# Dealing out VectorE work and moving loads and evictions in an FNet + GEGLU kernel on one core

## The chip, the cores and the metric

One core of one Trainium2 chip runs the kernel. The time is device microseconds for one execution. The profile is of another single execution on the same kind of core, and its times are microseconds from the start of its span. TensorE multiplies matrices; VectorE and ScalarE are the two engines that read its results out of PSUM; GpSimd does elementwise work on SBUF alone; SyncE and GpSimd also issue the transfers. Each engine works through its own instructions in order and waits for the others by semaphores.

## What is computed

`x` has 2048 rows (S) of 448 numbers (D). After a layer norm, `xn` goes two ways, and the two results are multiplied and added to `x`:

```python
xn = _layernorm(x)
a = einsum("bsd,ed->bse", xn, dft_hid_re)          # DFT along D, real part
b = einsum("bsd,ed->bse", xn, dft_hid_im)          # and imaginary part
s = einsum("ts,bse->bte", dft_seq_re, a) - einsum("ts,bse->bte", dft_seq_im, b)
g = silu((gelu(xn @ w_gate) * (xn @ w_up)) @ w_down)     # F = 1792
return x + s * g
```

## The kernel before

All is float32, but each operand is split for TensorE into a high part (rounded to the matmul's type) and a low part (the rest), so that a product takes two or three matmuls. `split` (L141) is that step: ScalarE copies the high part, VectorE subtracts it from the source. Several products are done as seven block products instead of eight, so that sums and differences of blocks have to be made first, of `x`, of weights and of DFT matrices.

The order is written out by hand (`tc.manual_schedule()`, L510): the order of the lines is the order on each engine. The stages:

1. **Start and first group of F, to 80 us.** `x` comes in four chunks c = 0..3 of 512 rows. For each, `stats` (L149) makes mean and variance on VectorE and ends with four tiny steps (`newton`, L164 to L170) on which `norm` waits; `turn_mm` (L184) transposes the normalized rows on TensorE, and `turn_split` (L196) brings them back as high part, low part (VectorE, L202) and a full copy `xf` (ScalarE, L201). With the first two blocks of F plain products are made: `gateup` (L388), `act`, and `down` (L423), whose results leave PSUM through ScalarE (L416, `po_out`) in two PSUM banks. `between` is a list of steps put between the four parts of a `down`.
2. **Combinations.** `combine(p, s)` (L207) makes from the `xf` blocks of a pair p of chunks (c = 2p and 2p+1) the four differences that the seven-product form needs: one memset and four subtractions of 128x512 per call, in place, each waiting for the one before. `t_places` and `v_places` (L221, L234) split them into tiles `t_lo` and `t_v`. For pair 0 both calls stand after the first `gateup` with all of c = 2 (L719), for pair 1 in the first unit of the next stage (L789).
3. **Twelve more blocks of F, 80 to 415 us.** `strassen` (L441) is one unit: a block of F with a pair of chunks, seven products into four PSUM banks `x1`..`x4`, with VectorE and ScalarE steps in between, and with lists of other steps (`preps`, and `dn` for pieces of the `down` of earlier units) at four places. `sums_s` (L291) makes the ten sums of a block's weights on GpSimd; its input comes by `load_s`, and `prep_s` splits the result. The first such weight block is loaded at L616, ahead of most of the start. `spill` and `fetch` write half of the transposed chunks 1 and 3 to DRAM, because `t_places` writes over them, and bring them back later. The summed results of the F blocks are kept in DRAM (`gs`), added there by transfers that GpSimd issues (L421).
4. **DFT along D, 415 to 492 us.** For each block k of 128 rows, in the order 0..13, 15, 14, `hid_mm` (L904) makes 22 matmuls into two PSUM banks. Eight banks are in turn, so that TensorE can be four blocks ahead. `hid_sums` (L928) evicts the two banks on ScalarE (L933, L934) into one of two buffers (`f_at`, L896: `a_t` for even k, `a_r[0]` for odd) and makes four sums on VectorE (L939 to L942); `hid_split` (L946) splits 128x1568 from there into the block's place `AT[k]` (ScalarE L951, VectorE L954). It is put off by one block (`behind`) up to k = 10 and done at once after that. Blocks 10 and 15 (`KP`) are only split (`hid_plain`, L919). In the same stage the four chunks of `gs` are fetched through the two halves of `a_st`, put through silu on ScalarE and stored back (L1038 to L1045): fetch of one chunk, in the next block its silu, its store, and the fetch of another. The first DFT matrices for the next stage are loaded by `load_c` (L982), summed by `sum_c` (VectorE, L1000 and L1001) and split by `prep_c` (L1005); the buffers of units 1 and 2 are the two halves of `a_r[0]`.
5. **DFT along S and output, 492 us to the end.** 112 units of 14 matmuls (`seven`, L1087) and 16 plain ones. Unit 0 begins when `hid_mm(14)` is through and uses the eight banks in the order in which `hid_mm` gave them back.

SyncE issues most loads in order, so a load whose buffer isn't free holds up those behind it.

Of the kernel before, what the change touches and what calls it, by code (L numbers as in the profile page):

```python
# [13 lines left out]
P = 128  # L14
S = 2048
D = 448
# [29 lines left out]
def fnet_geglu(ctx: ExitStack, tc: tile.TileContext, x, ca, ct, cp, et, wgu, wd, out):  # L46
# [66 lines left out]
    t_hl, t_lo, vt = [None, None], [], [None, None]  # L113
# [93 lines left out]
    def combine(p, s):  # L207


        (b11, b21), (b12, b22) = [  # L210
            [xfk(c, 2 * s + k) for k in range(2)] for c in (2 * p, 2 * p + 1)
        ]
        if s == 1:
            nc.gpsimd.memset(b22[64:], 0.0)
        nc.vector.tensor_sub(b11, b12, b11)
        nc.vector.tensor_sub(b12, b22, b12)
        nc.vector.tensor_sub(b22, b22, b11)
        n = 64 if s else P
        nc.vector.tensor_sub(b21[:n], b21[:n], b22[:n])

    def t_places(p):  # L221
# [4 lines left out]
        t_hl[p] = [list(zip(h, l)), None]  # L226
# [283 lines left out]
    with tc.manual_schedule():  # L510
# [105 lines left out]
        s_raw = load_s(GROUPS[1][0], 1)  # L616
# [33 lines left out]
        between = [lambda k=k: turn_split(*turn_mm(2, k)) for k in (1, 2, 3)]  # L650
        turn = between[0]
        between[0] = lambda: (turn(), l0())
# [15 lines left out]
        xp = [dram.tile([P, 2, 1024], F32, name=f"xp{p}") for p in range(2)]  # L668

        def x_half(p):  # L670
            return a_x[2 * p + 1].rearrange("p (a d) -> p a d", a=2)[:, :, :1024].bitcast(F32)

        def spill(p):
            nc.sync.dma_start(xp[p], x_half(p))

        def fetch(p):
            nc.sync.dma_start(x_half(p), xp[p])

# [3 lines left out]
        for c in (2, 3):  # L682
            if c == 2:
                draw = load_d(GROUPS[1], a_st[:, 2304:])
                spill(0)
# [3 lines left out]
            if c == 2:  # L689
# [3 lines left out]
                    lambda: (l0(), norm(3), turn(0)),  # L693
                    lambda: turn(1),
                    lambda: turn(2),
                ]
                between1 = [lambda: turn(3)]
                sums_s(s_raw, nc.gpsimd)
            else:
# [7 lines left out]
                v_split = v_places(0)  # L707
                between1 = [lambda: v_split(1), lambda: v_split(2)]
# [7 lines left out]
            if c == 2:  # L716
                h1()
                l1()
                combine(0, 0)  # L719
                combine(0, 1)  # L720
# [54 lines left out]
        for gi in range(1, len(GROUPS)):  # L775
# [7 lines left out]
            for bi, (i, p) in enumerate(zip((0, 1, 1, 0), sides)):  # L783
                preps = [[], [], [], []]
                if gi == 1 and bi == 0:
                    preps[0].append(lambda: (v_split(0), v_split(3)))
                if gi == 1 and bi < 2:
                    if bi == 0:
                        preps[1].append(lambda: combine(1, 0))  # L789
                        preps[3].append(lambda: combine(1, 1))  # L790
                    else:
                        tsp, vsp = t_places(1), v_places(1)
                        for n in range(4):
                            preps[n].append(lambda n=n: (tsp(n), vsp(n)))
# [14 lines left out]
                elif bi == 1:  # L809
                    if nxt:  # L810
# [4 lines left out]
                        else:  # L815
                            wdn, steps = prep_d(grp, draw)
                            for f in steps:
                                preps[0].append(f)
# [44 lines left out]
        def place(tag, n):  # L863
# [14 lines left out]
            7: lambda: a_x[0],  # L878
# [3 lines left out]
            12: lambda: a_x[1],  # L882
            13: lambda: place("st", 8 * D),
# [12 lines left out]
        def f_at(k):  # L896
            return (a_t if k % 2 == 0 else a_r[0])[:, : 8 * HD]
# [76 lines left out]
        def slot_at(m):  # L974
            return (
                lambda: (a_d[0][1], rest(a_x[0])),
# [41 lines left out]
        for k in [*range(14), 15, 14]:  # L1018
# [4 lines left out]
            if k == 14:  # L1023
                break
            if k in KP:
                hid_plain(k, ps, [rest(v) for v in ((vt[0], t_lo[0]), a_x[1:3])[k > 10]])
# [4 lines left out]
            if k not in KP:  # L1031
                behind.append(lambda k=k: hid_split(k)())
                if k > 10:
# [4 lines left out]
            for n, c in enumerate((2, 3, 0, 1)):  # L1038
                at = (3, 4, 6, 7)[n]
                if k == at:  # L1040
                    g_in[c] = stage(c)
                    nc.sync.dma_start(g_in[c], gv[:, 4 * c : 4 * c + 4])
                if k == at + 1:
                    nc.scalar.activation(g_in[c], g_in[c], AF.Silu)
                    nc.sync.dma_start(gv[:, 4 * c : 4 * c + 4], g_in[c])  # L1045
            if k == 8:
# [5 lines left out]
            if k == 13:  # L1052
                load_c(1)
                load_c(2)
                sum_c(3)
# [230 lines left out]
```

## Time and profile before

| | us |
|---|---|
| median of 3 runs (lowest, highest) | 803.74 (801.69, 804.31) |
| the profiled execution, whole | 805.21 |
| its span in the profile | 803.5 |
| TensorE matmuls busy | 773.8 |
| VectorE busy | 548.2 |
| ScalarE busy | 363.8 |
| GpSimd busy, DMA issues included | 175.7 |

TensorE has work nearly all the time, so what counts is where it is idle, and where its granted clock is below full: after some of the idle stretches it is 0.5 for a few microseconds. The transfers move 170 MB at 212 GB/s in the mean. A row of the timeline gives start, duration, engine, line, operation and tiles, and in brackets how long the engine had been idle and what ended that. Engine names in the rows: PE is TensorE, DVE VectorE, ACT ScalarE, POOL GpSimd, SP SyncE.

### The profile page before, as it was taken

The page shows a single profiled execution, that of the slowest core. Times are in us where ns is not written, and L with a number is a line of the kernel's source. Part 1 is how long each engine was busy: PE and PEld are TensorE (multiplying, and loading weights), DVE is VectorE, ACT ScalarE, POOL GpSimd, SP SyncE. Part 2 cuts the span into 40 slices and gives each one's busy share as a digit, 9 for nine tenths or more (in the row PEclk, how much of TensorE's full clock was granted, in tenths as well). Part 3 has the DMA queues.
Part 4 walks back from the last instruction along what each step waited for, and adds up shares of the span by engine and source line. Part 5 has one row for each costly group of instructions (what it writes and reads, how often), then busy time and mean ns, then how long its engine had stood idle before and what let it go on. Part 6 is the DMA issues. An engine that isn't in the chain of part 4 may idle for free. (4 is left out here: it accounts for less than half of the span.)

```text
span 803.5 us, 11376 instructions
## 1 busy us (share of the span) xinstructions
PE 773.8 (96%) x4044; PEld 692.5 (86%) x4044; DVE 548.2 (68%) x945; ACT 363.8 (45%) x538; POOL 175.7 (22%) x300
## 2 busy tenths in 40 slices
PE   9898899999999999999999996899999999999997
PEld 7787788888888888888889995799999999888996
DVE  7877778555565556455544546779787796969687
ACT  3684355344434444343444654444343444344341
POOL 2103006240321512401011000213232322213130
PEclk9999999999999999999999998799999999999999
DMA  8042445995878968865989860777796969596884
GB/s 307 12 161 112 163 136 151 269 203 119 235 142 219 276 115 230 172 138 110 300 173 262 340 258 17 230 271 235 270 309 209 343 196 360 177 314 210 292 246 187
DMA packets 61370, 170.05 MB, mean 212 GB/s; under 512 B 7424, under 2 KB 40064, under 8 KB 60416
## 3 DMA queue, kind: packets, MB, share of 16 engines
q1 hardware_dynamic: 47440, 108.17, 38.4%
q0 software_dynamic: 13728, 61.02, 33.1%
q8 instruction: 32, 0.52, 0.3%
q14 instruction: 26, 0.21, 0.1%
q10 hardware_dynamic: 144, 0.11, 0.0%
HBM read 127.21 MB, written 70.91 MB: 247 GB/s over the span
## 5 line engine op out<-in xcount | busy, mean ns | idle before, releaser
L432 PE MATMUL x<-xt,w 128*128 128x512 f32 x480 | 150.0, 393 | 3.0 <-DVE tmp L493 2.6
L432 PEld LDWEIGHTS x<-xt,w 128*128 128x128 f32 x480 | 90.5, 189 | 20.0 <-DVE tmp L493 3.0
L416 ACT ACTIVATE po_out<-po 128x448 f32<-128x448 f32 x112 | 60.1, 537 | 83.2 <-PE po L409 79.2
L409 PE MATMUL po<-wd0h,hs 128*128 128x448 f32 x256 | 82.7, 370 | 2.3 <-ACT po_out L416 2.3
L421 POOL DMA_DIRECT2D gs<-po_out x24 | 21.4, 890 | 218.8 <-ACT po_out L416 213.8
L915 PE MATMUL ab<-e,xt 128*128 128x448 f32 x288 | 68.8, 365 | 0.0
L409 PE MATMUL po<-wd,hs 128*128 128x448 f32 x288 | 66.0, 365 | 0.0
L432 PE MATMUL x<-t_v,w 128*128 128x512 f32 x216 | 61.1, 391 | 0.0
L409 PEld LDWEIGHTS po<-wd,hs 128*128 128x128 f32 x288 | 54.1, 188 | 6.6
L915 PEld LDWEIGHTS ab<-e,xt 128*128 128x128 f32 x288 | 54.1, 188 | 4.3
L409 PEld LDWEIGHTS po<-wd0h,hs 128*128 128x128 f32 x256 | 48.7, 190 | 7.7 <-ACT po_out L416 2.7
L1093 PE MATMUL p<-t_v,wd0l 128*128 128x448 f32 x112 | 39.3, 393 | 13.6 <-DVE xt L143 5.8
L994 POOL DMA_DIRECT2D raw<-sums x45 | 24.8, 551 | 110.3 <-DVE raw_d L1000 38.5
L432 PEld LDWEIGHTS x<-t_v,w 128*128 128x128 f32 x216 | 40.5, 188 | 8.8 <-DVE t_v L143 0.2
L409 PE MATMUL po<-wd0l,hs 128*128 128x448 f32 x128 | 47.4, 370 | 0.0
L142 ACT ACTIVATE e<-raw 128x896 fp32r<-128x896 f32 (+1 forms) x30 | 27.6, 921 | 36.9 <-DVE raw L1001 29.4
L487 ACT ACTIVATE hs<-tmp 128x512 fp32r<-128x512 f32 x24 | 15.2, 634 | 56.9 <-DVE tmp L485 56.9
L1093 PE MATMUL p<-w,e 128*128 128x448 f32 x112 | 38.6, 390 | 0.9 <-DMA w<-td 0.8
L432 PE MATMUL x<-t_lo,w 128*128 128x512 f32 x96 | 37.4, 389 | 0.0
L1093 PEld LDWEIGHTS p<-t_v,wd0l 128*128 128x128 f32 x112 | 21.4, 191 | 18.2 <-DVE xt L143 6.3
L1093 PE MATMUL p<-xt,e 128*128 128x448 f32 x112 | 36.1, 374 | 0.0
L994 POOL DMA_DIRECT2D tmp<-sums x39 | 21.4, 550 | 63.7 <-DVE xt L143 28.7
(298 smaller groups left out, 2007.1 us busy)
## 6 DMA issues: line engine op xcount, KB each, us to landing
gs<-po_out POOLq DMA_DIRECT2D x24, 896.0 KB, 8.5
sums<-ca SPq DMA_DIRECT2D x16, 896.0 KB, 10.7
sums<-ca POOLq DMA_DIRECT2D x16, 896.0 KB, 14.6
t_v<-td SPq DMA_DIRECT2D x24, 448.0 KB, 5.6
w<-td SPq DMA_DIRECT2D x24, 448.0 KB, 7.4
raw<-ct SPq DMA_DIRECT2D x45, 192.0 KB, 4.7
raw<-wgu SPq DMA_DIRECT2D x12, 640.0 KB, 4.2
tmp<-ct SPq DMA_DIRECT2D x39, 192.0 KB, 4.9
```

The source lines that it names most:

```text
L142: nc.scalar.activation(h, src, AF.Copy)
L409: nc.tensor.matmul(po[:, :D], hs[:, a, kk * P : (kk + 1) * P], wdn[b][:, i], start=n == 0, stop=n == 5,)
L416: nc.scalar.activation(out_[0][:, kk], po[:, :D], AF.Copy)
L421: nc.gpsimd.dma_start(gv[:, 4 * c : 4 * c + 4], out_[0], accum_op=ALU.add)
L432: nc.tensor.matmul(ps, a[i], b[j], start=first and n == 0, stop=n == 2, skip_group_check=True)
L487: nc.scalar.activation(hs[:, 0], g1, AF.Copy)
L915: nc.tensor.matmul(p[:, :D], a, b, start=n == 0, stop=n == len(mm) - 1)
L994: nc.gpsimd.dma_start(v[:, 4 * P : 6 * P], sums[j][:, KS.index(k)])
L1093: nc.tensor.matmul(ps[q][:, :D], h, v, start=u % UN == 0, stop=False, skip_group_check=True)
```

## The change

Three parts, in one diff.

- **Combinations.** `combine` now takes an engine and returns four steps. Pair 0 stays on VectorE, but its eight steps are taken one by one (`comb.pop(0)()`), after each of the turns of chunk 2 (k = 1, 2, 3) and chunk 3, the last one after `l1`. Pair 1 goes to GpSimd as a whole, at the head of the first unit, the s = 1 half first. The splits that follow are dealt out anew: those of pair 0 all before the first unit, those of pair 1 one at a time over the first two units and the head of the third.
- **Weight sums later.** `load_s` of the first summed weight block and its `sums_s` on GpSimd move from the start to behind `spill(0)`, just before the first `down`; `spill(0)` itself moves there from the third chunk.
- **End of the DFT-along-D stage.** The four chunks of `gs` get a place each (two in `a_st`, two in `g_in` over the tile of `x` chunk 0) and are fetched at k = 3, 4, 4, 5, with the silu three blocks later (6, 7, 7, 8). `load_c(0)` moves from k = 8 to k = 3. Block 13 uses buffer `a_t` instead of `a_r[0]`, block 11 is split one block later, blocks 12 and 13 change places in the tiles, and the loads of units 1 and 2 move from k = 13 to k = 12, with `sum_c(1)` ahead of block 15's split.

```diff
-    def combine(p, s):
+    def combine(p, s, eng):
...
+        def first_():
+            if s == 1:
+                nc.gpsimd.memset(b22[64:], 0.0)
+            eng.tensor_sub(b11, b12, b11)
+
+        return [
+            first_,
+            lambda: eng.tensor_sub(b12, b22, b12),
+            lambda: eng.tensor_sub(b22, b22, b11),
+            lambda: eng.tensor_sub(b21[:n], b21[:n], b22[:n]),
+        ]
...
         d_low()
-        s_raw = load_s(GROUPS[1][0], 1)
         load_x(3, 0, 4)
...
+        spill(0)
+        s_raw = load_s(GROUPS[1][0], 1)
+        sums_s(s_raw, nc.gpsimd)
+        comb = combine(0, 0, nc.vector) + combine(0, 1, nc.vector)
+
+        def turn2(k):
+            turn_split(*turn_mm(2, k))
+            if k == 1:
+                l0()
+            comb.pop(0)()
...
-                    lambda: (l0(), norm(3), turn(0)),
-                    lambda: turn(1),
-                    lambda: turn(2),
+                    lambda: (l0(), norm(3), turn(0), comb.pop(0)()),
+                    lambda: (turn(1), comb.pop(0)()),
+                    lambda: (turn(2), comb.pop(0)()),
                 ]
-                between1 = [lambda: turn(3)]
-                sums_s(s_raw, nc.gpsimd)
+                between1 = [lambda: (turn(3), comb.pop(0)())]
...
-                v_split = v_places(0)
-                between1 = [lambda: v_split(1), lambda: v_split(2)]
+                between1 = [lambda: v_split(0), lambda: v_split(3)]
...
-                combine(0, 0)
-                combine(0, 1)
+                comb.pop(0)()
+                v_split = v_places(0)
+                v_split(1)
+                v_split(2)
...
                 if gi == 1 and bi == 0:
-                    preps[0].append(lambda: (v_split(0), v_split(3)))
-                if gi == 1 and bi < 2:
-                    if bi == 0:
-                        preps[1].append(lambda: combine(1, 0))
-                        preps[3].append(lambda: combine(1, 1))
-                    else:
-                        tsp, vsp = t_places(1), v_places(1)
-                        for n in range(4):
-                            preps[n].append(lambda n=n: (tsp(n), vsp(n)))
+                    for f in combine(1, 1, nc.gpsimd) + combine(1, 0, nc.gpsimd):
+                        f()
+                    tsp, vsp = t_places(1), v_places(1)
+                    preps[0].append(lambda: vsp(3))
+                    preps[3].append(lambda: (vsp(1), tsp(1)))
+                if gi == 1 and bi == 1:
+                    for n, f, k in ((0, tsp, 2), (1, vsp, 2), (2, tsp, 0), (3, vsp, 0)):
+                        preps[n].append(lambda f=f, k=k: f(k))
+                if gi == 1 and bi == 2:
+                    tsp(3)
...
-            return (a_t if k % 2 == 0 else a_r[0])[:, : 8 * HD]
+            return (a_t if k % 2 == 0 or k > 12 else a_r[0])[:, : 8 * HD]
...
+            if k == 13:
+                behind.pop(0)()
+            if k == 15:
+                sum_c(1)
...
                 behind.append(lambda k=k: hid_split(k)())
-                if k > 10:
+                if k == 13:
                     behind.pop()()
...
-            for n, c in enumerate((2, 3, 0, 1)):
-                at = (3, 4, 6, 7)[n]
+            if k == 4:
+                x0 = sb.tile([P, 4096], F32, name="g_in", tag="x0")
+            for c, at, v in ((2, 3, (a_st, 0)), (3, 4, None), (0, 4, None), (1, 5, (a_st, 1))):
                 if k == at:
-                    g_in[c] = stage(c)
+                    v, i = v or (x0, int(c == 0))
+                    g_in[c] = part(v, 4 * D * i, 4, D)
                     nc.sync.dma_start(g_in[c], gv[:, 4 * c : 4 * c + 4])
-                if k == at + 1:
+                if k == at + 3:
                     nc.scalar.activation(g_in[c], g_in[c], AF.Silu)
                     nc.sync.dma_start(gv[:, 4 * c : 4 * c + 4], g_in[c])
-            if k == 8:
+            if k == 3:
                 raw_d0 = sb.tile([P, 2 * D], F32, name="raw_d0", tag="d0h")
                 load_c(0)
...
-            if k == 13:
+            if k == 12:
                 load_c(1)
                 load_c(2)
+            if k == 13:
                 sum_c(3)
...
-        sum_c(1)
         prep_c(1)
```

The first place is VectorE from the last turn of chunk 3 on; `xf_72` holds the blocks of pair 0, and the row with `gu_3_1` is the multiplication that the first `gateup` of chunk 3 waits for. Before:

```order
L202 TENSOR_TENSOR xt_69<-pt_3_661,xt_69 128x2x2x128
L383 TENSOR_TENSOR tmp<-tmp,gu_2_1_649 128x512
L385 TENSOR_TENSOR hs_79<-tmp,hs_79 128x512
L215 TENSOR_TENSOR xf_72<-xf_72 128x512
L216 TENSOR_TENSOR xf_72<-xf_72 128x512
L217 TENSOR_TENSOR xf_72<-xf_72 128x512
L219 TENSOR_TENSOR xf_72<-xf_72 128x512
L215 TENSOR_TENSOR xf_72<-xf_72 128x512
L216 TENSOR_TENSOR xf_72<-xf_72 128x512
L217 TENSOR_TENSOR xf_72<-xf_72 128x512
L219 TENSOR_TENSOR xf_72<-xf_72 64x512
L383 TENSOR_TENSOR tmp<-tmp,gu_3_1_696 128x512
```

The same place on VectorE now:

```order
L202 TENSOR_TENSOR xt_69<-pt_3_668,xt_69 128x2x2x128
L223 TENSOR_TENSOR xf_72<-xf_72 128x512
L389 TENSOR_TENSOR tmp<-tmp,gu_2_1_656 128x512
L391 TENSOR_TENSOR hs_79<-tmp,hs_79 128x512
L224 TENSOR_TENSOR xf_72<-xf_72 64x512
L143 TENSOR_TENSOR t_v_694<-xf_72,t_v_694 128x512 x2
L389 TENSOR_TENSOR tmp<-tmp,gu_3_1_701 128x512
```

Six of the eight combinations of pair 0 have gone to earlier places, and two splits stand ahead of the multiplication that stood behind it.

The second place is GpSimd behind the first weight sums, where `raw_74`, `xf_83` and `po_out` hold the blocks of pair 1 and `raw_75` the second weight block; now:

```order
L217 MEMSET xf_72 64x512
L217 MEMSET po_out 64x512
L218 TENSOR_TENSOR xf_83<-raw_74,xf_83 128x512
L222 TENSOR_TENSOR raw_74<-po_out,raw_74 128x512
L223 TENSOR_TENSOR po_out<-po_out,xf_83 128x512
L224 TENSOR_TENSOR xf_83<-xf_83,po_out 64x512
L218 TENSOR_TENSOR xf_83<-raw_74,xf_83 128x512
L222 TENSOR_TENSOR raw_74<-raw_74 128x512
L223 TENSOR_TENSOR raw_74<-raw_74,xf_83 128x512
L224 TENSOR_TENSOR xf_83<-xf_83,raw_74 128x512
L303 TENSOR_TENSOR raw_75<-raw_75 128x128
```

Before, the row of the weight sums followed the first memset directly; now eight subtractions stand ahead of it.

The third place is ScalarE at the end of the DFT-along-D stage, from block 11 to unit 1 (`raw_74` and `tmp` are the two buffers, `e_3015<-raw_74` is the split of unit 1's matrices). Before:

```order
L933 ACTIVATE raw_74<-ab_0_3654 128x2x224
L934 ACTIVATE raw_74<-ab_1_3666 128x2x224
L951 ACTIVATE xt_68<-raw_74 128x7x224
L933 ACTIVATE tmp<-ab_0_3686 128x2x224
L934 ACTIVATE tmp<-ab_1_3698 128x2x224
L951 ACTIVATE xt_67<-tmp 128x7x224
L933 ACTIVATE raw_74<-ab_0_3718 128x2x224
L934 ACTIVATE raw_74<-ab_1_3730 128x2x224
L951 ACTIVATE ts_st<-raw_74 128x7x224
L142 ACTIVATE xt_67<-ab_0_3757 128x448
L922 ACTIVATE xt_68<-ab_1_3769 128x448
L142 ACTIVATE e_3015<-raw_74 128x896
```

The same place on ScalarE now:

```order
L946 ACTIVATE raw_74<-ab_0_3655 128x2x224
L947 ACTIVATE raw_74<-ab_1_3667 128x2x224
L946 ACTIVATE tmp<-ab_0_3685 128x2x224
L947 ACTIVATE tmp<-ab_1_3697 128x2x224
L964 ACTIVATE xt_68<-raw_74 128x7x224
L964 ACTIVATE ts_st<-tmp 128x7x224
L946 ACTIVATE tmp<-ab_0_3721 128x2x224
L947 ACTIVATE tmp<-ab_1_3733 128x2x224
L964 ACTIVATE ts_x_3754<-tmp 128x7x224
L142 ACTIVATE ts_x_3754<-ab_0_3759 128x448
L935 ACTIVATE xt_68<-ab_1_3771 128x448
L142 ACTIVATE e_3015<-raw_74 128x896
```

Block 12 is evicted ahead of block 11's split, block 13 goes through `tmp` behind block 12, and so `raw_74` is given up for the loads of units 1 and 2 with block 11's split instead of block 13's.

42 lines of the change are left out of this document (16 added, 26 removed).

## The prediction

> **What bounds the kernel now.** I read the page first, then who TensorE waited for, then the stretches around those waits. The page's busy line and the waits of TensorE:
>
> ```profile
> PE 773.8 (96%) x4044; PEld 692.5 (86%) x4044; DVE 548.2 (68%) x945; ACT 363.8 (45%) x538; POOL 175.7 (22%) x300
> ...
> PE p L1093 <- DVE xt L143: 5.8, 1, 5.8
> PE p L1093 <- ACT tmp L933: 3.0, 1, 3.0
> PE pt L187 <- issue: 2.7, 1, 2.7
> PE x L432 <- DVE tmp L493: 2.6, 1, 2.6
> ...
> PE po L409 <- ACT po_out L416: 2.3, 1, 2.3
> PE p L1093 <- ACT raw L933: 2.1, 1, 2.1
> ```
>
> TensorE is the bound: 803.5 less 773.8 leaves some 30 us idle, and these six single waits are 18.5 of them. A wait can cost more than itself, since matmuls behind it can run at a lower clock. The stretches (duration, then busy us of PE, PEld, DVE, ACT, POOL, then PEclk):
>
> ```profile
> 20.70:23.60 2.90, 0.18 (x2) 0.10 (x2) 2.86 (x3) 0.72 (x1) 2.74 (x7) 1.00 0.05 14
> 23.60:28.70 5.10, 5.09 (x30) 4.88 (x31) 3.95 (x7) 2.90 (x5) 0.14 (x1) 0.67 0.00 0
> 67.70:75.10 7.40, 5.06 (x25) 4.36 (x24) 6.01 (x9) 3.48 (x7) 5.99 (x9) 1.00 0.00 0
> 94.30:98.40 4.10, 1.54 (x8) 0.96 (x6) 3.81 (x6) 0.08 (x1) 0.00 (x0) 1.00 0.30 124
> 98.40:104.00 5.60, 5.54 (x17) 4.33 (x17) 4.79 (x7) 5.36 (x11) 0.00 (x0) 0.70 0.02 4
> 414.00:492.30 78.30, 78.30 (x388) 72.58 (x387) 38.95 (x63) 41.30 (x51) 6.50 (x10) 1.00 0.79 244
> 492.30:516.60 24.30, 13.31 (x58) 11.37 (x58) 16.22 (x31) 11.10 (x14) 4.92 (x9) 0.65 0.36 110
> 516.60:572.00 55.40, 55.40 (x349) 52.74 (x348) 45.47 (x86) 24.32 (x27) 13.87 (x24) 1.00 0.85 287
> ```
>
> There are four holes: at 21, 72, 96 and 492 us. The one at 492, where the DFT along S begins, is by far the largest. At 55.40 / 349 = 0.159 us a matmul, its 58 matmuls need 9.2 us, and they took 24.3: 15.1 us lost, 11.0 of it idle and the rest at PEclk 0.5 to 0.65.
>
> **Part 1: the end of the DFT along D (gain 14.5).** TensorE itself never waits in 414 to 492; it runs ahead through eight banks while ScalarE falls behind. What holds ScalarE, and what that leads to at the end:
>
> ```profile
> ACT po_out L1044 <- DMA po_out<-gs: 12.9, 3, 6.5
> ...
> 477.49 0.53 ACT L933 ACTIVATE raw<-ab 128x448 f32<-128x448 f32 x1
> ...
> 485.86 0.53 ACT L933 ACTIVATE raw<-ab 128x448 f32<-128x448 f32 x1
> ...
> 488.50 1.52 ACT L951 ACTIVATE xt<-raw 128x1568 fp32r<-128x1568 f32 x1 [1.69 <-DVE raw L942]
> 489.93 0.52 ACT L933 ACTIVATE tmp<-ab 128x448 f32<-128x448 f32 x1
> ...
> 494.68 0.53 ACT L933 ACTIVATE raw<-ab 128x448 f32<-128x448 f32 x1
> ...
> 499.43 0.53 ACT L142 ACTIVATE xt<-ab 128x448 fp32r<-128x448 f32 x1
> ...
> 505.54 0.95 ACT L142 ACTIVATE e<-raw 128x896 fp32r<-128x896 f32 x1 [5.16 <-DVE raw L1001]
> 506.40 0.53 ACT L933 ACTIVATE tmp<-ab 128x448 f32<-128x448 f32 x1
> ...
> 465.57 0.77 PE L915 MATMUL ab<-e,xt 128*128 128x448 f32 x3
> ...
> 499.55 1.79 DVE L954 TENSOR_TENSOR ts_st<-raw,ts_st 128x1568 fp32r<-128x1568 f32 x1 [1.62 <-ACT ts_st L951]
> ```
>
> The silus wait 12.9 us for their fetches, each of which stands behind the store of the chunk before. Block 9, which TensorE finished at 465.57 (block 10 begins there), is evicted at 477.49: 11.9 us late. In the tail blocks 11, 12, 13 and 15 follow 4.1 to 4.8 us apart, no faster than TensorE makes them (78.30 / 388 = 0.202 us a matmul, 4.4 for the 22 of a block), so nothing is caught up. Then unit 1's matrices can only be loaded when block 13's split has left `raw` (499.55 + 1.79 = 501.3), their split stands until 505.54, and block 14's eviction is queued behind it, at 506.40. Unit 0 needs those banks.
>
> After the change the four fetches go out together. The one into slot 0 of `a_st` waits for the last accumulation, issued at 431.0, and the others stand behind it on SyncE, with `load_c(0)`:
>
> ```profile
> L421 POOL DMA_DIRECT2D gs<-po_out x24: 859/878/1041, 131.2 to 431.0; - x24
> ...
> DMA to landing us min/median/max: 7.1/8.5/15.4
> ```
>
> That landing is at 438 to 446. Four chunks of 0.92 MB at the 244 GB/s of this stage take 15 us, at full engines less: they are there by 453 to 461, and the silus stand behind the evictions of blocks 6, 7, 7 and 8 (455 to 465). So little of the 12.9 is left. ScalarE then loses only the table load and the second silu of block 7, some 2.8 us, and regains a part at block 10: I take 2 us late at block 9 instead of 11.9. From there by durations: block 11 evicted at 476.7, block 12 at 479.7 (TensorE makes it by 478.9), VectorE's lows of 11 and 12 at 482.9 and 484.7, loads of units 1 and 2 out at 483 instead of 501.4, block 13 through `tmp` by 490.3, block 15's lows by 492.5, unit 1's split at 492.5 to 494.6, block 14's eviction at 493.4 to 494.3. TensorE starts unit 0 at 492.3, needs block 15's banks at 493.6 and block 14's at 494.2, and unit 1 at 494.5: about 0.5 us is left of the 15.1. Units 4 and 5 load at 492.4, as soon as `e1` is free, and have the 56 x 0.159 = 8.9 us of units 0 to 3 for it. Gain 14.5, at worst 7 if fetches or the loads of units 1 and 2 come late. The new places and the exchange of blocks 12 and 13 change no duration.
>
> **Part 2: weight sums later (gain 3.4).** The tiny steps ahead of chunk 1's norm, and the same step where GpSimd is idle:
>
> ```profile
> 20.62 2.02 DVE L170 SCALAR_TENSOR_TENSOR sd<-sd 128x4 f32<-128x4 f32 x1
> ...
> 38.08 0.17 DVE L170 SCALAR_TENSOR_TENSOR sd<-sd 128x4 f32<-128x4 f32 x1
> ```
>
> L170 took 2.02 instead of 0.17 us while GpSimd ran the sums (2.74 busy in 20.70:23.60), on the path to the transposes. With the sums gone the hole shrinks by 1.85, and by 0.25 of its neighbours, to 0.6, and the clock of 0.67 over the next 5.1 us (1.7 us) should stay up. The sum is 3.8; I take 3.4, as the splits of chunk 1 come close to TensorE then. The sums now run behind `spill(0)`, by my estimate from about 36 on, beside work on VectorE that has some slack; what they cost there is in part 3.
>
> **Part 3: the combinations, hole at 72 (loss 1.0) and hole at 96 (gain 4.2).** At 72 `po` waits for ScalarE, which waits for a VectorE multiplication (L383) behind the eight combinations. VectorE from the first combination on, with two later rows of it; the one GpSimd subtraction of this size class; the stretch to which six combinations go; and ScalarE around the split of the second weight sums:
>
> ```profile
> 64.93 0.68 DVE L215 TENSOR_TENSOR xf<-xf 128x512 f32<-128x512 f32 x1
> ...
> 67.99 0.95 DVE L215 TENSOR_TENSOR xf<-xf 128x512 f32<-128x512 f32 x1
> ...
> 71.47 0.67 DVE L383 TENSOR_TENSOR tmp<-tmp,gu 128x512 f32<-128x512 f32 x1
> ...
> 97.62 0.67 DVE L493 TENSOR_TENSOR tmp<-tmp,x 128x512 f32<-128x512 f32 x1
> ...
> 128.03 2.26 DVE L503 TENSOR_TENSOR hs<-tmp,hs 128x512 fp32r<-128x512 f32 x1
> ...
> 72.17 0.63 ACT L384 ACTIVATE hs<-tmp 128x512 fp32r<-128x512 f32 x1 [2.56 <-DVE tmp L383]
> ...
> 8.49 1.85 POOL L279 TENSOR_TENSOR w<-raw,w 128x768 fp32r<-128x768 f32 x1 [7.17 <-DVE w L276]
> ...
> 40.00:62.70 22.70, 22.70 (x120) 19.54 (x119) 17.35 (x36) 19.68 (x39) 0.00 (x0) 1.00 0.41 148
> ...
> 83.78 0.94 ACT L315 ACTIVATE w<-raw 128x896 fp32r<-128x896 f32 x1
> 87.13 0.55 ACT L416 ACTIVATE po_out<-po 128x448 f32<-128x448 f32 x1 [2.40 <-issue]
> ```
>
> Eight took 71.47 - 64.93 = 6.5, 0.82 each; six go (-4.9), two splits come (+1.3). But the six now stand in 40 to 62.7, where VectorE has 22.70 - 17.35 = 5.4 us of idle for their 4.1, not always at the right place: its lows of chunks 2 and 3 slip by 0.5 to 2, which TensorE feels as some 1.4, and the multiplication gains less. From 62 GpSimd runs pair 1: 8 instructions of 128x512, by L279 at 1.85 x 512/768 = 1.24 us each, 10 us, longer with contention. Beside 128x128 sums a VectorE subtraction takes 0.95 instead of 0.68 in one place and 2.26 in another (L503), so a price from 0.3 to 1.6 each. About five stand ahead of the multiplication; I take 0.5 each, near the dense case, where VectorE always had the next one ready, as here. The wait at 72 stays at about 2.0 of 2.3; less 1.3 for the slips: -1.0, from +2 to -6.
>
> By the Trainium skill's page SBUF — State Buffer, section Who interferes with whom, a VectorE instruction with two SBUF inputs and a GpSimd instruction that reads SBUF shut each other out for a whole instruction. L503 agrees with it, the 0.95 at 67.99 less so; by that rule the five would wait up to 1.24 each and this part would be near its lower end.
>
> At 96 the hole waits for L493 at 97.62. VectorE has ten instructions fewer ahead of it in the first unit (eight combinations, two splits) and three splits more: 7 x 0.68 = 4.8 us earlier, against a hole of 2.6. Contention eats at most part of it, as GpSimd should be through by then. So the 2.6 go, and with them 0.30 of the 5.6 us behind at PEclk 0.70, 1.7: 4.2 us. The second weight sums now end on GpSimd at 82 to 86 by these prices; ScalarE's split of them (83.78) has 2.40 us of idle behind it. The later `tsp(3)` delays one load of `wd` by about 1 us, which may cost 0.3.
>
> The clock terms in parts 2 and 3 are 3.4 together. The Trainium skill's page TensorE: Matmul & The Clock Gate, section What's actually happening, gives an idle window of some 3.4 us before the clock halves; holes of 2.7 and 2.6 us did it here, so the rows decide. By that rule alone these terms could fail and the result would be about 786.
>
> **Sum.** 14.5 + 3.4 - 1.0 + 4.2 - 0.3 = 20.8 us. The profiled execution (805.21, span 803.5) would come to 784.4; it lay 1.5 above the median of 803.74, which gives 783.0.
>
> **Rivals.**
> - *GpSimd blocks VectorE in 62 to 86.* For it: L170 and L503. Against it: the dense case. Each blocked instruction pays 1.3 or more, the hole at 72 grows to 6 or 7 us with its clock loss, and 6 us of the gain go: 789. Chance 0.17.
> - *The end of the DFT along D stays bound.* If four fetches at once beside the `td` stores land after 465, or VectorE's chain through blocks 11 to 15 is longer than drawn, half of part 1 goes: 790. For it: a DMA share of 0.79 there, over 1.0 in single slices. Chance 0.14.
> - *Slower than before.* The same lock, but on all of the some 16 VectorE instructions with two SBUF inputs in 62 to 90, each at the 1.6 of L503, all on the path: 25 us against 20.8, so 808. It decides from 1.3 each with none hidden; VectorE has several microseconds of idle there. Chance 0.03.
> - *The hole at 72 closes as well* and the slips are hidden: 779. Chance 0.06.
> - *No change worth measuring*: TensorE could be held by something else at 492, such as the first loads. Nothing shows that. Chance 0.03.
>
> **Numbers.** The forecast has 0.57. The range goes from 777 (part 3 at +2, no remainder in parts 1 and 2) to 792 (either of the first two rivals and a bit more). 0.3% is 2.4 us, about what a measurement of this kernel can tell from no change. Faster 0.94, same 0.03, slower 0.03.
>
> **What would show it.** Right: no idle of ScalarE at the silus, PEclk at full from 485 to 520 and under 2 us idle there; L170 ahead of chunk 1 at 0.17; no hole in the first unit. Wrong: ScalarE still over 6 us behind at block 9, or a wait of TensorE over 4 us in 60 to 90 behind VectorE subtractions that take over 1.5 us.

## The result and the profile after

The kernel after takes 783.58 us (median of 4 runs, 782.86 to 784.53) against 802.72 (800.11 to 804.31): the ratio is 0.9765, with a 95% interval of 0.9734 to 0.9797. Its profiled execution took 782.91, with a span of 781.1. That is 22.4 us less span than in the profile before. The medians lie only 19.1 apart, since the profiled execution before was 2.5 above its median and the one after 0.7 below; by the ratio it is 18.9.

The busy line of the page after, and the largest waits of TensorE:

```profile
PE 766.0 (98%) x4044; PEld 686.4 (88%) x4044; DVE 545.3 (70%) x937; ACT 363.8 (47%) x538; POOL 189.1 (24%) x308
```

```profile
PE p L1112 <- DVE cc L1209: 3.6, 4, 1.0
PE po L415 <- ACT po_out L422: 3.1, 1, 3.1
...
PE pt L187 <- issue: 0.4, 1, 0.4
```

Of the six single waits before, five are gone or down to 0.4. The one for `po_out` at 72 us has grown, from 2.3 to 3.1. The stretches that answer to those of before (duration, then busy us of PE, PEld, DVE, ACT, POOL, then PEclk):

```profile
23.60:28.70 5.10, 4.98 (x38) 4.50 (x37) 3.84 (x7) 3.92 (x8) 0.00 (x0) 1.00 0.00 2
...
72.20:76.00 3.80, 3.80 (x18) 3.25 (x19) 3.80 (x5) 3.45 (x7) 3.80 (x6) 1.00 0.26 109
...
485.60:494.60 9.00, 9.00 (x57) 8.31 (x57) 6.49 (x13) 5.31 (x8) 3.09 (x6) 1.00 0.60 182
```

The start of the last stage has no idle at all now (9.00 of 9.00, clock 1.00), and the clock behind the first transposes of chunk 1 is full. Where the 22.4 came from is seen by setting the start of each TensorE instruction against that of the same instruction before (the order is the same). This lead, with the times of before, is 3.4 us at instruction 133 (27.55), 2.4 ahead of the hole at 72 and 1.7 at its end, 6.3 behind the hole at 96, 6.8 at 131, 21.9 at 511 and 22.4 at the end.

ScalarE at the silus and at the end of the DFT along D:

```profile
452.62 3.29 ACT L1063 ACTIVATE g_in<-g_in 128x1792 f32<-128x1792 f32 x2
...
458.05 1.71 ACT L1063 ACTIVATE po_out<-po_out 128x1792 f32<-128x1792 f32 x1
460.10 0.55 ACT L946 ACTIVATE raw<-ab 128x448 f32<-128x448 f32 x1 [0.33 <-DVE xt L967]
...
485.43 0.95 ACT L142 ACTIVATE e<-raw 128x896 fp32r<-128x896 f32 x1 [3.01 <-PE ab L928]
486.29 0.53 ACT L946 ACTIVATE tmp<-ab 128x448 f32<-128x448 f32 x1
```

No silu waits for its fetch. Block 9, finished by TensorE at 458.7, is evicted at 460.10, 1.4 us late. Before, 11.9. At 485.43 ScalarE waits for TensorE, whose matmuls of block 14 read `e` until then: ScalarE is no longer the one that is late.

Around the hole at 72, VectorE and GpSimd:

```profile
60.51 1.18 DVE L223 TENSOR_TENSOR xf<-xf 128x512 f32<-128x512 f32 x1
...
62.99 1.77 DVE L391 TENSOR_TENSOR hs<-tmp,hs 128x512 fp32r<-128x512 f32 x1 [0.70 <-ACT hs L390]
64.69 1.78 DVE L224 TENSOR_TENSOR xf<-xf 64x512 f32<-64x512 f32 x1
66.40 3.46 DVE L143 TENSOR_TENSOR t_v<-xf,t_v 128x512 fp32r<-128x512 f32 x2
69.79 0.67 DVE L389 TENSOR_TENSOR tmp<-tmp,gu 128x512 f32<-128x512 f32 x1
```

```profile
61.23 1.62 POOL L222 TENSOR_TENSOR raw<-po_out,raw 128x512 f32<-128x512 f32 x1
64.30 1.62 POOL L224 TENSOR_TENSOR xf<-xf,po_out 64x512 f32<-64x512 f32 x1
```

Four VectorE instructions with two SBUF inputs take 1.77 us instead of 0.69 beside GpSimd's. The multiplication at 69.79, which reads one input from PSUM, takes its usual 0.67.

### The profile page after: what moved, and what is told of

It reads as the page before. It is cut to its first block, busy times and chain, and to the rows that moved or that the text cites. A ratio compares the mean times of both kernels' runs of the same rounds, so it can differ in the third digit from the quotient of the medians.

```text
span 781.1 us, 11376 instructions
## 1 busy us (share of the span) xinstructions
PE 766.0 (98%) x4044; PEld 686.4 (88%) x4044; DVE 545.3 (70%) x937; ACT 363.8 (47%) x538; POOL 189.1 (24%) x308
## 4 chain that ended last, share of the span: by engine, by line
PE 69%; DVE 15%; DMA 10%; issue 3%; ACT 1%; SPq 0%; DVEq 0%; ACTq 0%
PE x L438 23%; PE po L415 16%; PE ab L928 9%; PE p L1112 8%; PE x L445 4%; PE p L1115 4%; DVE xt L143 4%; DVE e L143 3%; DMA w<-td 3%; PE gu L361 3%; DMA raw<-ct 2%; DMA tmp<-ct 2%; DMA raw<-wgu 1%; DMA raw_d<-ct 1%; DVE cc L1150 1%
## 5 line engine op out<-in xcount | busy, mean ns | idle before, releaser
L1112 PE MATMUL p<-t_v,wd0l 128*128 128x448 f32 x112 | 37.5, 380 | 3.6 <-DVE cc L1209 3.6
L1112 PE MATMUL p<-w,e 128*128 128x448 f32 x112 | 36.6, 375 | 0.1
L323 DVE TENSOR_TENSOR w<-raw,w 128x512 fp32r<-128x512 f32 (+1 forms) x24 | 21.3, 889 | 19.9 <-ACT w L321 19.9
L143 DVE TENSOR_TENSOR e<-raw,e 128x896 fp32r<-128x896 f32 (+1 forms) x30 | 31.4, 1047 | 4.3 <-ACT e L142 4.0
## 6 DMA issues: line engine op xcount, KB each, us to landing
sums<-ca POOLq DMA_DIRECT2D x16, 896.0 KB, 14.5
```

What stands on the lines that cost most here:

```text
L143: nc.vector.tensor_sub(l, src, h)
L1112: nc.tensor.matmul(ps[q][:, :D], h, v, start=u % UN == 0, stop=False, skip_group_check=True)
```

## The experiments

The theory after the result: three parts that add up, and a hole at 72 that is left because GpSimd holds up VectorE there (the lock: while GpSimd is in an instruction that reads SBUF, one of VectorE's with two SBUF inputs has to stand, and the other way round). All kernels in one table; the ratio is to the kernel before on the same chip, with its 95% interval.

| run | what | median us | ratio |
|---|---|---|---|
| e1_dend | before + end of DFT along D | 791.20 | 0.9847 (0.9819 to 0.9875) |
| e2_sums | before + weight sums later | 799.87 | 0.9950 (0.9928 to 0.9973) |
| e3_comb | before + combinations | 800.24 | 0.9961 (0.9943 to 0.9980) |
| e6_fetch | after, old order at the end of D | 787.41 | 0.9793 (0.9764 to 0.9823) |
| e7_tail | after, old fetches | 792.29 | 0.9859 (0.9834 to 0.9884) |
| e4_dve | after, pair 1 on VectorE | 783.26 | 0.9761 (0.9741 to 0.9782) |
| e5_sumsfirst | after, second weight sums first | 779.65 | 0.9722 (0.9699 to 0.9744) |
| e8_halves | after, GpSimd in halves | 779.03 | 0.9705 (0.9678 to 0.9731) |
| e5_again | e5_sumsfirst again | 781.76 | 0.9717 (0.9693 to 0.9741) |
| after_again | after again | 783.88 | 0.9765 (0.9739 to 0.9790) |
| e9_chain | after, halves in a chain | 782.11 | 0.9760 (0.9735 to 0.9785) |
| e10_both | sums first, halves in a chain | 779.53 | 0.9719 (0.9699 to 0.9740) |

### Each part alone

**e1_dend**: only the hunks of the diff from `AT` on.

> The kernel before with the part on the end of the DFT along D alone. Theory (three parts that add up: 15.1 us here, 3.4 for the weight sums, some 2.7 net for the combinations): 15.1 us faster than before, and the holes at 21, 72 and 96 us as they were. Rival (the parts need each other, as part 1 gets its slack from an earlier start): under 12 or over 18 us.

TensorE's waits, and the stretch from where the last stage begins:

```profile
PE x L432 <- DVE tmp L493: 2.5, 1, 2.5
PE po L409 <- ACT po_out L416: 2.4, 1, 2.4
PE pt L187 <- issue: 2.2, 1, 2.2
```

```profile
492.00:516.60 24.60, 24.60 (x157) 23.20 (x156) 21.55 (x41) 14.39 (x17) 6.45 (x12) 1.00 0.81 269
```

The first three holes stand as they did, and the fourth is shut without any lead from the earlier stages: 157 matmuls where 58 ran in a stretch of about that length before. Against the trace of before the lead is 0.35 ahead of the hole, 15.1 at 511 and 15.5 just behind it. The ratio gives 12.3 (10.0 to 14.5): of the difference, 2.0 is that the profiled execution before lay above the median of 803.21 of its 23 runs in this comparison, and 1.4 is given back in the last stage. That the parts need each other is not borne out by the trace; the interval of the time alone would reach below the rival's 12.

**e2_sums**: `load_s`, `sums_s` and `spill(0)` moved as in the diff, the rest as before.

> The kernel before with the weight sums and the spill later, and nothing else. Theory: 3.4 us faster, L170 ahead of chunk 1 at 0.17 us, the TensorE clock in 23 to 28 us at full; with the sums now beside VectorE in 36 to 60 us nothing shows on TensorE there. Rival (the sums only move their contention to the later stretch): L170 at 0.17, but 1 us or more is lost again before 72 us, and the gain is under 2.4 us.

The last tiny step ahead of chunk 1's norm on VectorE, and the stretch from the transposes on:

```profile
20.11 0.17 DVE L170 SCALAR_TENSOR_TENSOR sd<-sd 128x4 f32<-128x4 f32 x1
```

```profile
21.00:26.10 5.10, 4.98 (x39) 4.51 (x40) 3.81 (x7) 3.40 (x7) 0.00 (x0) 1.00 0.00 2
```

L170 is back at 0.17 and the clock at 1.00. The lead is 3.8 at the instruction that stood at 27.55 before, 3.6 at 41 and 3.4 from 60 to 97, with the sums running at 35.5 to 40.4: at most 0.3 was given back there. By the ratio 4.0 us (2.2 to 5.8). One thing more stands in this trace: behind the hole at 96 (2.54 here) the clock stayed full, and then TensorE waited 1.69 for VectorE's L471, at 100.67. The lead is 3.4 on both sides of it, so what the halved clock cost there before was lost to VectorE here: in the first unit VectorE sets the pace.

**e3_comb**: only the combinations and splits, with the steps of `prep_d` one place later (an edit of the whole change that the diff above leaves out).

> The kernel before with the combinations and splits dealt out anew and pair 1 on GpSimd; the weight sums and the end of the DFT along D as before. Theory: 2.7 us faster (4.5 from the hole at 96, 1.8 lost before it), the wait at 72 us about 3.1 with VectorE's instructions of 128x512 at 1.77 us there. Rival (the loss before 72 comes from the weight sums that now run beside VectorE, not from the combinations): 4 us or more faster and a wait at 72 of 2.3 or less.

The wait of TensorE at 72:

```profile
PE po L415 <- ACT po_out L422: 3.1, 1, 3.1
```

3.1 us faster (1.6 to 4.6) by the ratio, with the wait at 72 at 3.1 and none in the first unit. So the growth of that hole belongs to the combinations, not to the weight sums beside VectorE. The three gains, 12.3 + 4.0 + 3.1 = 19.4, add up to the 18.9 of the whole change, well within their intervals.

### The end of the DFT along D: fetches or order

**e6_fetch** keeps the four places, the early `load_c(0)` and the new tiles of the blocks, and takes back the rest of that part:

```diff
-            return (a_t if k % 2 == 0 or k > 12 else a_r[0])[:, : 8 * HD]
+            return (a_t if k % 2 == 0 else a_r[0])[:, : 8 * HD]
...
-            if k == 13:
-                behind.pop(0)()
-            if k == 15:
-                sum_c(1)
...
-                if k == 13:
+                if k > 10:
                     behind.pop()()
...
-            if k == 12:
+            if k == 13:
                 load_c(1)
                 load_c(2)
...
         load_c(5)
+        sum_c(1)
         prep_c(1)
```

> The kernel after, but of its edits to the DFT along D only the fetch into four places is kept: block 13 in the second buffer, blocks 11 and 12 split at once, the loads of units 1 and 2 and the sum for unit 1 where they were before. Theory (being on time on ScalarE carries part 1, and the order at the end is a finish): 2 to 4 us slower than the kernel after, so 15.5 to 17.5 us faster than the kernel before, block 9 evicted about 1.3 us after TensorE made it. Rival (the loads of units 1 and 2 behind block 13's split carry it): 7 us or more slower than the kernel after, with a hole of over 5 us where unit 1 begins.

**e7_tail** is the opposite: the fetches, their places, `load_c(0)` and the tiles of the blocks as before, the new order at the end.

> The kernel after, but with the chain of fetches of the kernel before (each behind a store, the silu in the next block) and the new order at the end. Theory (being on time on ScalarE carries part 1): ScalarE is over 10 us late at block 9 again, and the gain over before is 8 to 13 us, so 7 to 12 slower than the kernel after. Rival (the new order at the end carries it): within 4 us of the kernel after.

ScalarE in e6_fetch, block 9 and the end of the stage:

```profile
461.15 0.54 ACT L946 ACTIVATE raw<-ab 128x448 f32<-128x448 f32 x1 [0.33 <-DVE xt L967]
...
489.43 0.95 ACT L142 ACTIVATE e<-raw 128x896 fp32r<-128x896 f32 x1 [5.30 <-DVE raw L1014]
490.28 0.53 ACT L946 ACTIVATE tmp<-ab 128x448 f32<-128x448 f32 x1
```

In e7_tail, the last silu and block 9:

```profile
470.62 1.70 ACT L1061 ACTIVATE po_out<-po_out 128x1792 f32<-128x1792 f32 x1 [6.12 <-DMA po_out<-gs]
472.22 0.52 ACT L946 ACTIVATE raw<-ab 128x448 f32<-128x448 f32 x1
```

With the fetches alone block 9 is 1.4 us late (finished at 459.7), but the split of unit 1 stands 5.30 us and block 14's eviction is held behind it until 490.28; TensorE, done with block 14 at 486.6, loses 4.1 there against the kernel after, by the start of its instructions. With the order alone block 9 is 11.1 late (finished at 461.1), and 8.8 are lost at the same place. So of the 15.1 the fetches alone bring about 11 and the order alone about 6.3; together that is some 2 more than both bring, so they overlap. By the medians e6_fetch is 3.8 and e7_tail 8.7 slower than the kernel after, by the ratios 2.2 and 7.5: both as the theory had it.

### The hole at 72: the lock, or VectorE's own work

**e4_dve**:

```diff
-                    for f in combine(1, 1, nc.gpsimd) + combine(1, 0, nc.gpsimd):
-                        f()
+                    cmb1 = combine(1, 1, nc.vector) + combine(1, 0, nc.vector)
+                    for n in range(4):
+                        preps[n] += cmb1[2 * n : 2 * n + 2]
...
-                    preps[0].append(lambda: vsp(3))
+                    preps[2].append(lambda: vsp(3))
```

> The kernel after with pair 1's combinations on VectorE, two at each of the four places of the first unit, and no combination on GpSimd. Theory (GpSimd's subtractions hold up VectorE's): the wait at 72 us falls from 3.1 to under 0.6, VectorE's 128x512 there take 0.68 us again; the eight subtractions bring back a hole in the first unit of up to 3 us, so that the time lies within 2.5 us of the kernel after. Rival (the hole at 72 is the slips from the six earlier combinations): the wait at 72 stays over 2 us, and the time is 3 us or more over the kernel after.

VectorE ahead of the multiplication, and TensorE in the first unit:

```profile
62.30 0.69 DVE L391 TENSOR_TENSOR hs<-tmp,hs 128x512 fp32r<-128x512 f32 x1 [0.70 <-ACT hs L390]
62.91 0.68 DVE L224 TENSOR_TENSOR xf<-xf 64x512 f32<-64x512 f32 x1
63.52 1.28 DVE L143 TENSOR_TENSOR t_v<-xf,t_v 128x512 fp32r<-128x512 f32 x2
65.29 0.69 DVE L389 TENSOR_TENSOR tmp<-tmp,gu 128x512 f32<-128x512 f32 x1 [0.50 <-PE gu L361]
```

```profile
93.42 0.61 PE L438 MATMUL x<-xt,w 128*128 128x512 f32 x1 [2.60 <-DVE tmp L499]
```

The same four instructions are back at 0.69, the multiplication starts 4.5 us earlier and no wait is left at 72. The eight subtractions in the first unit bring back its hole, 2.60 us and the halved clock behind it, and the time is that of the kernel after. Against this placing on VectorE, pair 1 on GpSimd is thus worth nothing in the change as it stands: it shuts one hole and opens another.

**e5_sumsfirst**: GpSimd makes the second weight sums first, while their input lands, and pair 1 behind them.

```diff
+                    sums_s(s_raw2, nc.gpsimd)
                     for f in combine(1, 1, nc.gpsimd) + combine(1, 0, nc.gpsimd):
                         f()
...
-                    preps[0].append(lambda: vsp(3))
+                    preps[2].append(lambda: vsp(3))
...
-                        sums_s(s_raw2, nc.gpsimd)
                         n_raw[-1] = s_raw2
```

> The kernel after, with GpSimd doing the second weight sums ahead of pair 1's combinations (their load lands about 63 to 67 us), and the split that reads a combination's result two places later. Theory (the lock of the 128x512 subtractions makes the hole at 72): the wait at 72 shrinks to under 1.5 us, since small sums run there in place of them; the large ones go beside the first unit, where VectorE has slack; 1 to 3 us faster than the kernel after. Rival (any GpSimd work beside VectorE costs as much): wait at 72 at 2.5 or more, time within 1 us of the kernel after or above it.

> The kernel of the run with the second weight sums ahead of pair 1's combinations, once more, on one chip with the kernel after. Theory: 3 to 4.5 us faster than the kernel after, since both the wait at 72 us and the one in the first unit are gone in its profile. Rival (chance of the clock in a few runs): within 1.5 us.

VectorE in e5_sumsfirst:

```profile
63.40 1.56 DVE L143 TENSOR_TENSOR t_v<-xf,t_v 128x512 fp32r<-128x512 f32 x2
...
67.92 0.96 DVE L143 TENSOR_TENSOR t_lo<-xf,xt 128x512 fp32r<-128x512 f32 x1 [2.07 <-ACT xt L142]
...
73.68 3.47 DVE L143 TENSOR_TENSOR t_v<-xf,t_v 128x512 fp32r<-128x512 f32 x2
```

TensorE waits neither at 72 nor in the first unit: its instruction at 72.12 comes 3.6 us earlier, and 3.3 of that is kept at 94. Beside the small sums VectorE pays 0.27 (0.96), beside the large ones 1.05 as before, but from 69.86 on, where it has slack. The first run lies 3.5 below the kernel after by the ratios, a little more than the 1 to 3 expected. Again, on one chip with the kernel after, the ratios are 0.9717 and 0.9765, 3.9 us; the medians lie 2.1 apart. That is at or a little under what was expected then and over the rival's bound of 1.5, with intervals that just touch.

**e8_halves**: each subtraction on GpSimd as two of 128x256.

```diff
+        def sub(o, a, b):
+            w = 256 if eng is nc.gpsimd else 512
+            for i in range(0, 512, w):
+                eng.tensor_sub(o[:, i : i + w], a[:, i : i + w], b[:, i : i + w])
```

> The kernel after with each of GpSimd's subtractions for pair 1 made as two of 128x256, the same bytes in twice the instructions. Theory (one instruction of either engine shuts out the other's until it is through, and they take turns): VectorE's 128x512 beside them take about 1.2 us instead of 1.77, GpSimd's halves about 1.3 each where VectorE is dense, the wait at 72 us falls from 3.1 to about 1, and the time is 1 to 2.5 us below the kernel after. Rival (both run at the same time and share the bytes that SBUF gives): VectorE's stay at 1.7 or more, GpSimd's halves take about 0.85, the wait at 72 stays near 3.1 and the time the same within 1 us.

VectorE, then GpSimd:

```profile
62.06 1.24 DVE L396 TENSOR_TENSOR hs<-tmp,hs 128x512 fp32r<-128x512 f32 x1 [0.70 <-ACT hs L395]
63.23 1.21 DVE L223 TENSOR_TENSOR xf<-xf 64x512 f32<-64x512 f32 x1
64.36 2.36 DVE L143 TENSOR_TENSOR t_v<-xf,t_v 128x512 fp32r<-128x512 f32 x2
66.65 0.67 DVE L394 TENSOR_TENSOR tmp<-tmp,gu 128x512 f32<-128x512 f32 x1
68.54 5.32 DVE L143 TENSOR_TENSOR t_lo<-xf,xt 128x512 fp32r<-128x512 f32 x1 [1.22 <-ACT xt L142]
```

```profile
68.68 1.42 POOL L223 TENSOR_TENSOR raw<-raw 128x256 f32<-128x256 f32 x2
70.07 1.42 POOL L223 TENSOR_TENSOR raw<-raw,xf 128x256 f32<-128x256 f32 x2
71.46 1.43 POOL L223 TENSOR_TENSOR xf<-xf,raw 128x256 f32<-128x256 f32 x2
72.85 0.45 POOL L308 TENSOR_TENSOR raw<-raw 128x128 f32<-128x128 f32 x1
```

VectorE's 128x512 fell from 1.77 to 1.21 with the same bytes, GpSimd's halves took 1.18 beside them instead of the 0.85 of a shared rate, and the wait at 72 fell to 0.4: the engines take turns by whole instructions, and do not share a rate. The Trainium skill's page "SBUF — State Buffer", section "Who interferes with whom", states such an exclusive lock for the two engines, and the runs agree with it. The time is 4.9 us below the kernel after (779.03 against 783.88), twice what was expected. By the starts of TensorE's instructions 2.7 of it stand from 100 to 520 us against the trace of the kernel after, whose clock stayed full behind the wait, and 3.9 against that of after_again, where it halved; the rest arises in the last stage, whose code is the same and in which after and after_again, one kernel, differ by up to 1.5 as well. But one split took 5.32 us: it came after a pause of VectorE, and got in only when GpSimd was through the six halves at 68.68 and the first weight sum. From 60 to 100 us no wait of TensorE is over 0.41.

**e9_chain** orders the halves so that nearly each reads or writes a block that the one just before it used (`combine` takes the columns as `cs`), **e10_both** puts the sums first as well:

```diff
-                    for f in combine(1, 1, nc.gpsimd) + combine(1, 0, nc.gpsimd):
-                        f()
+                    for s in (1, 0):
+                        for cs in (slice(0, 256), slice(256, 512)):
+                            for f in combine(1, s, nc.gpsimd, cs):
+                                f()
```

> The kernel after with GpSimd's subtractions in halves, all four steps of the left half and then all four of the right, so that nearly each waits for the one just before it (in the run with halves the two halves of a step stood side by side, and one VectorE split that came after a pause took 5.32 us, until GpSimd was through with eight instructions). Theory (VectorE gets in where GpSimd's next instruction waits for the one before): no VectorE instruction of 128x512 over 1.5 us in 60 to 75 us, no wait at 72, within 1 us of the run with halves or below it. Rival (an instruction that comes after a pause waits whatever GpSimd's instructions depend on): one of over 2.5 us again.

> The second weight sums ahead of pair 1's combinations, and these in halves in a chain. Theory (both remove the same wait, and behind it TensorE is the bound): no wait of TensorE in 60 to 100 us, and within 1 us of the run with the sums first alone. Rival (VectorE's splits in the first unit are still late because of the 1.77 us ones): 1.5 us or more faster than that run.

e9_chain, GpSimd's first instruction, VectorE, and TensorE:

```profile
54.74 0.31 POOL L217 MEMSET po_out<- 64x256 f32 x1 [13.60 <-ACT po_out L201]
```

```profile
59.81 1.68 DVE L323 TENSOR_TENSOR w<-raw,w 128x896 fp32r<-128x896 f32 x1
...
69.96 0.84 DVE L143 TENSOR_TENSOR t_lo<-xf,xt 128x512 fp32r<-128x512 f32 x1 [1.22 <-ACT xt L142]
70.72 1.22 DVE L391 TENSOR_TENSOR hs<-tmp,hs 128x512 fp32r<-128x512 f32 x1
```

```profile
62.15 1.20 PE L361 MATMUL gu<-xt,w 128*128 128x512 f32 x4 [1.31 <-DVE xt L202]
```

From 60 to 75 us no VectorE instruction of 128x512 is over 1.22 us now, even after the pause at 69.96, so what was forecast of the long one came true, though by that one instruction. On the time it missed: 782.11, 3.1 above e8_halves (4.4 by the ratios). The left half of a chunk is ready two turns earlier, so GpSimd began at 54.74 instead of 59.14, beside a weight split that then took 1.68 (1.09 in e5_sumsfirst), and TensorE waited 1.31 for the last low of chunk 3. That explains a third of the miss: by TensorE's starts e9_chain is 1.0 behind e8_halves from 100 to 520 us, and the other 2.2 of the two traces come in the last stage, whose code is the same; their cause is not shown. With the sums first (e10_both, 779.53) GpSimd does not begin early, and the time is that of e5_sumsfirst, with one wait of 0.6 in the first unit where none was expected. Beside e8_halves these are the best; the runs don't separate them.

## Why the prediction was right, step by step

- **End of the DFT along D** (14.5): 15.1 between the two traces, nothing left of the hole. Block 9 was 1.4 late, where 2 was taken. e6_fetch and e7_tail show both halves of the argument at work: the silus off their chain, and the loads of units 1 and 2 off block 13's split.
- **Weight sums later** (3.4): 3.4 in the trace, 4.0 (2.2 to 5.8) alone. L170 and the clock came out as written: 0.17, and 1.00 in 23.60:28.70.
- **Hole at 72** (-1.0): -1.75, of which 1.0 are the slips ahead of it (1.3 taken) and 0.75 the longer wait. This is the term that was mis-sized, and the step is "I take 0.5 each, near the dense case". The row it was taken from stood beside 128x128 sums, 0.46 us alone; beside 128x512 the price was 1.08 each, near the upper end of 1.24 that the text gave (1.23 by its own row). The wait grew to 3.1 instead of shrinking to 2.0. Four instructions paid that and one 0.5 (L223, 1.18 at 60.51), 4.8 us in place of 2.5. It was luck of the profiled execution that the clock did not halve behind the hole: in after_again it did, and 1.5 more went.
- **Hole at 96** (+4.2): +4.5. GpSimd was through at 79.9, and nothing of its work was felt in the first unit. The text put 1.7 of the gain on the clock; e2_sums lost as much there at full clock, to a wait for VectorE, so it is VectorE's earlier work that brought all of it.
- **Late load of `wd`** (-0.3): nothing lost; a wait of 0.3 before 131 went as well, +0.6.
- The sum: 15.1 + 3.4 - 1.75 + 4.5 + 0.6 + 0.5 in the last stage = 22.4, against 20.8. That the median forecast, 783.0, lies within 0.6 of 783.58 is in part luck: the two traces differ by 1.6 more than 20.8, the medians by 1.7 less, and the median before came out 1.0 lower than the one the forecast was taken from.
- The lower end of the range, 777, is not what its terms give: 3 more from part 3 and about 1 from the remainders of parts 1 and 2 make 779. Nothing else hung on it.
- The rival of GpSimd blocking VectorE had the mechanism right and the place; its price of 6 us would have needed the lock on more of the path, and the clock. The sign of being wrong that the text named (a wait over 4 us behind subtractions over 1.5) was met in the subtractions, 1.77, not in the wait, 3.1.

## What to carry to other kernels

Price an instruction on VectorE with two SBUF inputs beside GpSimd by the length of GpSimd's instruction, not by a row beside shorter ones: where VectorE was dense it paid 1.08, 0.52 and 0.26 us beside GpSimd instructions that take 1.27, 0.73 and 0.46 alone, each time some 0.2 less than the whole. So long GpSimd instructions belong where VectorE has slack, or are cut into shorter ones. Look also at where a GpSimd step becomes free to begin: cutting it can start it earlier, in a worse place. And when a stage ends in a tangle of buffers, look upstream first: about 11 of the 15 us could be had by the fetches alone, which had made ScalarE late 30 us before. A clock term behind a wait of 2 to 3 us is a chance and not a price: the next section shows on what it hangs.

## What was not expected of the hardware

**The clock after a wait.** Before, waits of 2.6 and 2.7 us were followed by a clock of 0.70 and 0.67. In the profiled execution of after a wait of 3.1 was followed by 1.00. The stretch behind that wait in the kernel after, then in after_again (the same kernel, the same wait of 3.1 us), then in e7_tail (3.1 us too):

```profile
72.20:78.00 5.80, 5.80 (x26) 4.91 (x27) 5.80 (x7) 4.05 (x8) 5.80 (x8) 1.00 0.48 181
```

```profile
72.20:78.00 5.80, 5.80 (x21) 4.74 (x20) 5.51 (x7) 3.65 (x8) 5.80 (x7) 0.71 0.48 181
```

```profile
72.20:78.00 5.80, 5.80 (x16) 4.73 (x16) 5.36 (x6) 3.11 (x7) 5.71 (x9) 0.52 0.39 158
```

1.00, 0.71 and 0.52 behind the same wait: the length of an idle stretch alone doesn't decide, and what TensorE lost is 0, 1.5 or 2.8 us. What does decide can be read from the traces. In all of them the clock changes on a fixed beat: a stretch at half clock between two at full lasts 3.41 us or a whole multiple of it (at most 17.07, in the kernel before from 495.5 on). The beat that holds most of the wait, in the same three traces:

```profile
67.49:70.91 3.42, 1.53 (x8) 1.07 (x6) 2.97 (x3) 0.42 (x1) 3.26 (x3) 1.00 0.00 0
```

```profile
69.56:72.97 3.41, 1.21 (x6) 1.14 (x7) 2.19 (x3) 2.85 (x6) 3.33 (x4) 1.00 0.00 0
```

```profile
67.51:70.92 3.41, 1.17 (x6) 0.75 (x4) 2.62 (x3) 0.76 (x2) 3.25 (x3) 1.00 0.00 0
```

In the kernel after 1.9 us of the wait fall in one beat and the rest in the next; TensorE is busy for 1.53 and 2.20 us of them, and the clock stays up. In the other two 2.2 us fall in one beat, 1.21 and 1.17 are left busy, and the half clock begins with the next beat, at 72.97 and 70.92. Before the change 0.95 and 1.24 us were busy in the beats ahead of the two halvings (24.49 and 99.58). Taken over all fourteen traces there is no exception: of the beats at full clock, the 27 that were followed by half had TensorE busy for at most 1.39 us, and all others for at least 1.53. Back to full it went only behind a beat that was busy for 3.19 or more; in e7_tail the first beat at half had 2.54, so a second one followed. So where a wait falls on the beat decides. This is read off the traces; no run varied it on purpose.

The Trainium skill's page "TensorE: Matmul & The Clock Gate", section "What's actually happening", states that activity is watched in windows of some 3.4 us that run free of the program, and the beat of 3.41 agrees with it. Its table has the clock halved after an idle window; here beats that were busy for up to 1.39 us were enough, and the measurement decides.

**Who gets in.** In e8_halves a VectorE split that came after a pause of 1.22 us waited 5.32 us through seven of GpSimd's instructions; in e9_chain the same split took 0.84. Before the change L503 took 2.26 and L170 2.02 beside small sums, and both got in where GpSimd itself stood still for 0.08 us, ahead of its ninth sum (at 129.74 and 22.61). This would fit a turn that passes only where GpSimd's next instruction has to wait for its own last one. But in e8_halves L396 came after a pause too, of 0.70, and got in after one half (62.06); VectorE instructions that follow each other closely got their turn after every half; and the 5.32 itself ended between two sums without such a standstill. The cause stays open.
